# Weight pieces of two chunks' columns for half of the rows, in an attention and SwiGLU kernel

## Chip, cores and metric

The kernel runs on one core of a Trainium2 chip. The metric is the device time of one execution in microseconds (us), the median of three runs; lower is better. The core has five engines with instruction queues of their own: PE (TensorE, with its weight loads listed as PEld), DVE (VectorE), ACT (ScalarE), POOL (GpSimd) and SP (SyncE, which here only starts DMAs).

## What is computed

Block-causal attention over q, k, v of 8 batches, 8 heads, 576 positions and 64 dimensions (float32), then a SwiGLU layer on the 4,608 x 512 result. The three weights are float64.

```python
scores = q @ k.T / sqrt(64)             # hidden where the key's block of 64 is later than the query's
attn = softmax(scores); x = attn @ v    # heads side by side: x is 4608 x 512
g, val = x @ w_gate, x @ w_val          # 512 x 1536 each, float64
out = (g * sigmoid(g) * val) @ w_out    # 1536 x 512, float64
```

## The kernel before

**Work and tiles.** Attention goes by batch and by pairs of heads: scores on PE (L436 in plain float32 for the first two batches, L562 and L646 in split parts after them), copies and masks on ACT (L454, L459), maxima on DVE (L700) and POOL (L704), exponentials on ACT (L732), and the product with v on PE (L772). The first two batches are cut into smaller stretches (`FIRST`). Feed-forward goes by 18 tiles of 256 rows of x; a tile takes the 1,536 columns in 12 chunks of 128, in pairs of chunks. For a pair, `up` makes gate and value products (L1095 to L1097: three products of high and low float32 parts for each of the four row groups d of 128), ACT and DVE make the gated result (L1128 to L1144), and L1186 to L1188 multiply by w_out. Tiles 0 and 1 run between the attention of the first batches, while the weights still come in; `MIXED` gives the order in which their pairs are made.

**Weights.** `weight(i, kind)` brings one piece: chunk i of w_gate, w_val or w_out (kind 0, 1, 2), 36 pieces of 512 KB. A piece of w_gate or w_val is 128 columns for all 512 rows: 128 partitions, four runs of 128 float64 each, so 512 packets of 1,024 bytes. It lands in one of five `wo` buffers (L939). The two words of each float64 are joined into float32 by ACT (L954, L958) and DVE (L963, L968), then split into a high part (ACT, L973) and a low part (DVE, L976), each one instruction of 128x512. They go to `v_all` for w_val, to `g_even` or `g_odd` for w_gate of an even or odd chunk. The loads are chained in the order of chunks and kinds. Copies of the converted w_out are stored to DRAM (L992, L995) for the later tiles.

**Borrowed room.** The copies of w_out chunks 0 to 5 lie, until they are stored and tile 0 (and for chunks 0 to 3 tile 1) has read them, in the room of w_gate chunks 10, 11, 8, 9 and w_val chunks 10, 11 (`AWAY`). The list `before_place` makes the high part of those later pieces wait for that.

**Order.** The order of all instructions is fixed at build time. `add` and `dma` give each task an engine, an estimated cost, a rank and the tasks and buffers that it waits for; `in_order` walks through time and gives an idle engine the ready task of the lowest rank. `PIECES` holds ranks of the weight pieces, `AHEAD` those of some loads, `FIRST` those of attention of batches 0 and 1, `SIDE` those of the products of tiles 0 and 1. A later tile has 10 + its first row / 576, and attention of batch b has 10 + b - `LEAD`, with the score products `EAGER` earlier. `spare` is how far ahead of a buffer's release a task may be queued. Every engine then works through its own list in that order and stands still at an instruction whose inputs aren't there.

Of the kernel before, what the change touches and what calls it, by code (L numbers as in the profile page):

```python
# [7 lines left out]
F32 = mybir.dt.float32  # L8
F32R = mybir.dt.float32r
I32 = mybir.dt.int32  # L10
F16 = mybir.dt.float16
AF = mybir.ActivationFunctionType
ALU = mybir.AluOpType
# [5 lines left out]
def kernel(  # L19
# [17 lines left out]
    nc = tc.nc  # L37
    B, H, S, D = q.shape
    NT, DM = out.shape
    DFF = w_gate.shape[1]  # L40
    P = 128
# [4 lines left out]
    SP = NKC * P  # L46
    NDC = DM // P
# [2 lines left out]
    XT = 256  # L50


    LEAD, EAGER = 1.69, 0.3

    SUMS = 2


    ROWS = (2,)
    MIXED = (0, 0, 1, 1, 0, 1, 0, 0, 1, 1, 0, 1)

    FINE = 4

    AHEAD = {(0, 1): 2.01, (0, 2): 2.07, (1, 0): 2.03, (1, 1): 2.5, (1, 2): 2.5}
    LATER = 0.6

    PIECES = [
        (2.46, 1.85, 2.03),
        (4.86, 5.95, 3.63),
        (4.60, 2.52, 1.48),
        (3.87, 3.06, 5.35),  # L70
        (1.93, 3.59, 2.41),
        (5.14, 6.91, 5.83),
        (3.58, 2.93, 2.93),
        (0.08, 1.36, 0.92),
        (-2.10, -5.86, -4.34),
        (-7.48, -5.87, -3.82),
        (-7.64, -9.14, -8.44),
        (-12.11, -9.50, -10.88),
    ]

    SIDE = (2.98, 4.19)

    PATIENCE = 10.0

    FIRST = {
        0: [(0, 256, (-4.21, 2.41, 2.06, 2.12)), (256, 576, (-2.91, -2.07, -6.62, -4.11))],
        1: [(0, 256, (4.02, 3.94, 4.16, 3.63)), (256, 576, (-2.93, 1.90, 2.56, 4.50))],
    }
    TILES = [XT] * (NT // XT)

# [1 line left out]
    wide = w_gate.dtype != F32  # L92
# [56 lines left out]
    def add(engine, cost, rank, fn, after=(), bufs=(), port=False, mode=""):  # L149


        t = Task(engine, cost, rank, fn, after, bufs, port, mode)
        for a in after:
            if a is not None:
                a.next.append(t)
                t.waits += 1
        for u in bufs:
            u.left += 1
        t.n = len(tasks)
        tasks.append(t)  # L160
        return t


    def act_us(n, psum=False, more=0.0):
        return (0.05 if psum else 0.093) + n * 0.000833 + more

    def dve_us(n, one=False):
        return 0.07 + n * (0.00052 if one else 0.00104)
# [8 lines left out]
    def dma(rank, size, fn, after=(), bufs=(), n=1, engine="SP", packet=1024):  # L177

        t = add(engine, 0.5 * n, rank, fn, after, bufs)
        t.moves = size / packet * (9.0 + 0.0385 * packet) / 16e3  # L180
        return t
# [21 lines left out]
    def w_at(which, x, i):  # L203

        if which:
            return v_all[x][:, :, i * P : (i + 1) * P]
        return (g_odd if i % 2 else g_even)[x][:, :, i // 2 * P : (i // 2 + 1) * P]
# [100 lines left out]
    for i in range(7):  # L308
        n = 2**i
# [31 lines left out]
    def attention(R, b, h, a, e, early, bufs, lane):  # L341
# [1 line left out]

        Q = R - (0.1 if early else EAGER)
        visits, runs = STRETCHES[a, e]
        if b < 2:

# [546 lines left out]
    def words(ap):  # L896
        return ap.bitcast(I32) if wide else ap
# [11 lines left out]
    def weight(i, kind):  # L909

        R = PIECES[i][kind]
        raw = Buf("wo", "raw")
        away = AWAY.get(i) if kind == 2 else None  # L920
        wo = Buf("wo", "out") if kind == 2 and not away else None
        fs = slice(i * P, (i + 1) * P)

        parts = 1 if wo else NDC

        def part(j):
            if wo:
                return wo[0][:, j : j + 1]
            which, c = away or (kind, i)
            return w_at(which, j, c)  # L930

        def load():
            view = raw[0].rearrange("p (n m) -> p n m", n=NDC if kind < 2 else 1)
            if kind < 2:
                fs = slice(i * P * (1 + wide), (i + 1) * P * (1 + wide))
                src = words((w_gate, w_val)[kind])[:, fs].rearrange("(c p) f -> p c f", p=P)
            else:
                src = words(w_out)[i * P : (i + 1) * P, :].rearrange("p (n m) -> p n m", n=1)
            nc.sync.dma_start(out=view, in_=src)  # L939

        t = chain["w"] = dma(AHEAD.get((i, kind), R), 5e5, load, [chain["w"]], [raw], packet=1024 if kind < 2 else 4096)
        bufs = [raw, wo] if wo else [raw]

        def words_of(j):
            w = raw[0].rearrange("p (n t) -> p n t", t=1 + wide)[:, :, j]
            return w.rearrange("p (n m) -> p n m", n=parts)

        y = Buf("ob", "signs") if wide else None


        def signs():
            w = words_of(1).bitcast(F32)
            to = y[0].rearrange("p (n m) t -> p n m t", n=parts)[:, :, :, 1]
            nc.scalar.mul(to, w, 2.0**-60)  # L954

        def scaled():
            w = words_of(1).bitcast(F32)
            nc.scalar.mul(w, w, 2.0**-112)  # L958


        def fraction():
            s = y[0].rearrange("p m t -> p (m t)").bitcast(I32).rearrange("p (n m) -> p n m", n=parts)
            nc.vector.scalar_tensor_tensor(  # L963
                words_of(0), words_of(0), 29, s, ALU.logical_shift_right, ALU.bitwise_or
            )

        def exponent():
            nc.vector.scalar_tensor_tensor(  # L968
                words_of(0), words_of(1), 3, words_of(0), ALU.logical_shift_left, ALU.bitwise_or
            )  # L970

        def high():
            nc.scalar.copy(part(0), words_of(0).bitcast(F32))  # L973

        def low():
            nc.vector.tensor_tensor(  # L976
                part(1), words_of(0).bitcast(F32), part(0).bitcast(F32), ALU.subtract
            )

        if wide:  # L980
            t = add("ACT", act_us(DM, more=0.13), R, signs, [t], [raw, y])
            f = add("DVE", dve_us(DM), R, fraction, [t], [raw, y], True)
            t = add("ACT", act_us(DM, more=0.06), R, scaled, [t], [raw])
            t = add("DVE", dve_us(DM), R, exponent, [t, f], [raw], True)
        t = w_high[i, kind] = add("ACT", act_us(DM, more=0.04), R, high, [t], bufs)
        t = add("DVE", dve_us(DM), R, low, [t], bufs, True)
        if kind == 2:
            w_kept[i] = t, wo, part

            def store():  # L990
                if wo:
                    nc.sync.dma_start(out=wo_d[i], in_=wo[0].bitcast(F32))  # L992
                    return
                for j in range(2):
                    nc.sync.dma_start(  # L995
                        out=wo_d[i][:, j].rearrange("p (n m) -> p n m", n=parts), in_=part(j).bitcast(F32)
                    )

            t = dma(R, 5e5, store, [t], [wo] if wo else [], 2 if away else 1, packet=512 if away else 4096)
            if away:  # L1000
                before_place.append((t, away))
        w_done[i, kind] = t
# [58 lines left out]
    def feed_forward(j, t0, w, xs):  # L1061
# [19 lines left out]
        def up(i, which, prev):  # L1081

            ps = Buf("gv")
            ts = up_done[0]
            for y in range(2):

                for ds in [range(NDC)] if j >= FINE else [[d] for d in range(NDC)]:

                    def products(ds=ds, y=y):
                        hi, lo = (w_at(which, k, i + y) for k in range(2))  # L1090
                        o = ps[0][:, y * w : (y + 1) * w]
                        for d in ds:
                            xhi, xlo = (xs[d][1][k] for k in range(2))
                            first, last = d == 0, d == NDC - 1
                            nc.tensor.matmul(o, lhsT=hi[:, d], rhs=xhi[:, 0:w], start=first, stop=False)  # L1095
                            nc.tensor.matmul(o, lhsT=hi[:, d], rhs=xlo[:, 0:w], start=False, stop=False)  # L1096
                            nc.tensor.matmul(o, lhsT=lo[:, d], rhs=xhi[:, 0:w], start=False, stop=last)  # L1097

                    ts = add(
                        "PE",  # L1100
                        mm_us(w, w, w) * len(ds),
                        rank(i),
                        products,
                        [ts, *(xs[d][0] for d in ds), w_done[i + y, which]],
                        [ps, *(xs[d][1] for d in ds)],
                    )
                    ts.prev = prev
                    prev = ts if j >= FINE else None
            chain["up"] = up_done[0] = ts
            return ps, ts  # L1110
# [161 lines left out]
        next(tiles[j], None)  # L1272

    for t, (which, c) in before_place:
        t.next.append(w_high[c, which])
        w_high[c, which].waits += 1


    IN_TURN = set(
# [3 lines left out]
    def in_order():  # L1283
# [14 lines left out]
        now = queue = 0.0  # L1298
        mode, last = "", None

        spare = {"PE": 2.12, "DVE": 0.32, "ACT": 0.75, "POOL": 0.0, "SP": 0.0}

        def place(t, by):

# [104 lines left out]
```

## Time and profile before

| what | us |
|---|---|
| three runs, median (lowest to highest) | 1179.26 (1177.92 to 1181.79) |
| the profiled execution | 1177.14 |
| its span, first to last instruction | 1175.3 |
| PE busy in the span | 1149.0 |
| DVE, ACT, POOL busy | 754.4, 625.0, 323.7 |

The profiled execution is 1.84 us longer than its span and 2.12 us under the median. PE is busy for 98% of the span, so the time is PE's work and its gaps. The mean granted clock of PE is 0.994 of full speed.

### The profile page before, as it was taken

What the parts mean: (1) busy time and instruction counts of PE and PEld (TensorE: products, weight loads), DVE (VectorE), ACT (ScalarE), POOL (GpSimd) and SP (SyncE); (2) the same over time, 40 slices, a digit from 0 to 9 for tenths busy, and PEclk for the clock granted to TensorE, in tenths of its full rate; (3) what the DMA queues carried; (4) which work ended last, traced back from release to release, by engine and by line L of the source; (5) the groups of instructions that cost most, each with busy time, mean ns of one, the idle gap of its engine ahead of it and who ended that gap; (6) DMA issues with size and microseconds to landing.
All of it is one profiled execution on the core that took longest, in us unless ns stands there. A gap on an engine that the chain in (4) does not pass through costs nothing.

```text
span 1175.3 us, 21803 instructions
## 1 busy us (share of the span) xinstructions
PE 1149.0 (98%) x8512; PEld 1026.9 (87%) x8512; DVE 754.4 (64%) x1226; ACT 625.0 (53%) x1122; POOL 323.7 (28%) x139
## 2 busy tenths in 40 slices
PE   6889999999999999999999999999999999999998
PEld 4568778898898989998999899899989899999997
DVE  5988988575887668768585867686857423323222
ACT  6889877546573837474656565656555212112111
POOL 3222100144535251335233433343324200000000
PEclk9899999999999999999999999999999999999999
DMA  8758756766554756755665565656553536453442
GB/s 213 200 150 217 197 187 227 209 177 166 170 145 139 198 165 167 218 148 158 177 173 153 155 175 146 191 157 173 151 182 125 160 136 190 145 168 135 144 132 102
DMA packets 266983, 197.40 MB, mean 168 GB/s; under 512 B 195264, under 2 KB 231376, under 8 KB 266880
## 3 DMA queue, kind: packets, MB, share of 16 engines
q1 hardware_dynamic: 264304, 195.29, 57.0%
q8 instruction: 67, 1.10, 0.4%
q10 hardware_dynamic: 2576, 0.72, 0.3%
q14 instruction: 36, 0.29, 0.1%
HBM read 171.57 MB, written 24.38 MB: 167 GB/s over the span
## 4 chain that ended last, share of the span: by engine, by line
PE 84%; DVE 6%; ACT 5%; DMA 2%; issue 1%; POOL 1%; SPq 1%; DVEq 0%; ACTq 0%; POOLq 0%
PE gv L1095 16%; PE gv L1097 15%; PE gv L1096 15%; PE po L1186 7%; PE po L1187 7%; PE po L1188 7%; PE at L772 7%; PE at L562 5%; DVE mx L700 1%; DMA wo<-in_moe_w_out_dram 1%; DVE sc L728 1%; PE po L772 1%; PE at L436 1%; ACT sc L732 1%; PE at L646 1%
## 5 line engine op out<-in xcount | busy, mean ns | idle before, releaser
L704 POOL PARTITION_ALL_REDUCE mx<-mx x80 | 142.9, 1833 | 400.4 <-DVE mx L700 126.3
L1095 PE MATMUL gv<-xhl,v_all 128*128 128x256 f32 x864 | 242.3, 280 | 0.8 <-DVE t L1131 0.7
L1097 PE MATMUL gv<-xhl,v_all 128*128 128x256 f32 x864 | 239.7, 277 | 0.2 <-DVE v_all L976 0.2
L1096 PE MATMUL gv<-xhl,v_all 128*128 128x256 f32 x864 | 239.5, 277 | 0.0
L823 POOL PARTITION_ALL_REDUCE mx<-mx x48 | 178.4, 3764 | 195.7 <-DVE mx L700 167.5
L1131 DVE SCALAR_TENSOR_TENSOR t<-t,gv 128x512 f32<-128x512 f32 x108 | 74.0, 685 | 190.4 <-ACT t L1128 190.2
L1095 PEld LDWEIGHTS gv<-xhl,v_all 128*128 128x128 f32 x864 | 162.1, 188 | 5.1 <-issue 2.5
L1096 PEld LDWEIGHTS gv<-xhl,v_all 128*128 128x128 f32 x864 | 162.3, 188 | 0.6
L1097 PEld LDWEIGHTS gv<-xhl,v_all 128*128 128x128 f32 x864 | 162.2, 188 | 0.4 <-DVE v_all L976 0.4
L1128 ACT ACTIVATE t<-gv 128x512 f32<-128x512 f32 x108 | 64.7, 599 | 173.4 <-PE gv L1097 173.3
L1186 PE MATMUL po<-wo,hhl 128*128 128x512 f32 x372 | 147.4, 396 | 0.2 <-ACT ob L1213 0.2
L1187 PE MATMUL po<-wo,hhl 128*128 128x512 f32 x372 | 145.7, 392 | 0.0
L1188 PE MATMUL po<-wo,hhl 128*128 128x512 f32 x372 | 145.1, 390 | 0.2 <-DVE hhl L1144 0.2
L1141 ACT CAST hhl<-t 128x512 fp32r<-128x512 f32 x108 | 67.1, 621 | 130.3 <-DVE t L1136 128.0
L732 ACT ACTIVATE sc<-sc 128x1024 f32<-128x1024 f32 (+3 forms) x104 | 105.9, 1031 | 52.2 <-DVE sc L728 51.5
L1136 DVE SCALAR_TENSOR_TENSOR t<-t,gv 128x512 f32<-128x512 f32 x108 | 73.8, 684 | 90.1 <-PE gv L1097 89.4
L728 DVE TENSOR_TENSOR sc<-sc,mx 128x640 f32<-128x640 f32 (+6 forms) x168 | 122.1, 766 | 13.9 <-POOL mx L704 13.8
L1095 PE MATMUL gv<-xhl,g_even 128*128 128x256 f32 x432 | 123.5, 286 | 0.0
L1097 PE MATMUL gv<-xhl,g_even 128*128 128x256 f32 x432 | 122.2, 283 | 0.0
L1096 PE MATMUL gv<-xhl,g_even 128*128 128x256 f32 x432 | 122.1, 283 | 0.0
L1095 PE MATMUL gv<-xhl,g_odd 128*128 128x256 f32 x432 | 120.8, 280 | 0.0
L1144 DVE TENSOR_TENSOR hhl<-t,hhl 128x512 fp32r<-128x512 f32 x108 | 91.2, 845 | 45.3 <-ACT hhl L1141 44.8
(172 smaller groups left out, 2445.4 us busy)
## 6 DMA issues: line engine op xcount, KB each, us to landing
wo<-wo_d SPq DMA_DIRECT2D x200, 512.0 KB
out_dram<-ob SPq DMA_DIRECT2D x35, 256.0 KB
v<-in_v_dram SPq DMA_DIRECT2D x64, 128.0 KB
xt<-x_d SPq DMA_DIRECT2D x64, 128.0 KB
rt<-r_d SPq DMA_DIRECT2D x128, 64.0 KB
qk<-in_q_dram SPq DMA_DIRECT2D x112, 72.0 KB
qk<-in_k_dram SPq DMA_DIRECT2D x104, 72.0 KB
x_d<-xu SPq DMA_DIRECT2D x24, 288.0 KB
```

Source lines behind the costliest of these rows:

```text
L704: nc.gpsimd.partition_all_reduce(m, m, channels=P, reduce_op=bass_isa.ReduceOp.max)
L728: nc.vector.tensor_tensor(piece(c), scores_of(c), m, ALU.subtract)
L732: nc.scalar.activation(x, x, AF.Exp)
L772: nc.tensor.matmul(ps[0][own(x), 1 - i if sums else i, q0 - s0 : s1 - s0], lhsT=ones if sums else vt[0][:, 2 * lane + c, own(x)], rhs=sc[0 ...
L823: nc.gpsimd.partition_all_reduce(m, m, channels=P, reduce_op=bass_isa.ReduceOp.add)
L1095: nc.tensor.matmul(o, lhsT=hi[:, d], rhs=xhi[:, 0:w], start=first, stop=False)
L1096: nc.tensor.matmul(o, lhsT=hi[:, d], rhs=xlo[:, 0:w], start=False, stop=False)
L1097: nc.tensor.matmul(o, lhsT=lo[:, d], rhs=xhi[:, 0:w], start=False, stop=last)
L1144: nc.vector.tensor_tensor(hh[1][:, 0:n], t[0][:, 0:n], hh[0][:, 0:n].bitcast(F32), ALU.subtract)
L1186: nc.tensor.matmul(po, lhsT=hi, rhs=whi, start=i + y == 0, stop=False)
L1187: nc.tensor.matmul(po, lhsT=hi, rhs=wlo, start=False, stop=False)
L1188: nc.tensor.matmul(po, lhsT=lo, rhs=whi, start=False, stop=i + y == NFC - 1)
```

## The change

Pieces of w_gate and w_val are cut in the other direction: piece i has the columns of both chunks of its pair (256 columns), for the first 256 rows of x's dimension if i is even and the last 256 if it is odd. A piece still has 512 KB, now in 256 packets of 2,048 bytes. For w_gate, the two chunks lie in two tiles, so the high part becomes two ACT instructions and the low part two DVE instructions, of 128x256 each; for w_val they stay one each. Products of row groups d = 0, 1 of either chunk wait for the even piece, those of d = 2, 3 for the odd one. The pieces that come into borrowed room wait for both copies of the pair. The ranks, `MIXED`, `LEAD` and `spare` have new values.

```diff
-    LEAD, EAGER = 1.69, 0.3
+    LEAD, EAGER = 1.50189, 0.3
-    MIXED = (0, 0, 1, 1, 0, 1, 0, 0, 1, 1, 0, 1)
+    MIXED = (0, 0, 1, 1, 0, 0, 1, 0, 1, 1, 1, 0)
-    AHEAD = {(0, 1): 2.01, (0, 2): 2.07, (1, 0): 2.03, (1, 1): 2.5, (1, 2): 2.5}
+    AHEAD = {(0, 1): 2.07, (0, 2): 2.07, (1, 0): 2.07, (1, 1): 2.0, (1, 2): 2.0}
...
-    SIDE = (2.98, 4.19)
+    SIDE = (10.4268, 5.41963)
...
-        Q = R - (0.1 if early else EAGER)
+        Q = R - (0.3 if early else EAGER)
...
+        two = NDC // 2
+        c0, ds = i - i % 2, slice(i % 2 * two, (i % 2 + 1) * two)
...
+        def split(j):
+            if kind == 2:
+                return [(part(j), slice(0, parts), slice(None))]
+            if kind == 1:
+                return [(v_all[j][:, ds, c0 * P : (c0 + 2) * P], slice(0, two), slice(None))]
+            return [(w_at(0, j, c0 + y)[:, ds], slice(0, two), slice(y * P, (y + 1) * P)) for y in range(2)]
...
-                fs = slice(i * P * (1 + wide), (i + 1) * P * (1 + wide))
-                src = words((w_gate, w_val)[kind])[:, fs].rearrange("(c p) f -> p c f", p=P)
+                fs = slice(c0 * P * (1 + wide), (c0 + 2) * P * (1 + wide))
+                src = words((w_gate, w_val)[kind])[:, fs].rearrange("(c p) f -> p c f", p=P)[:, ds]
...
-            nc.scalar.copy(part(0), words_of(0).bitcast(F32))
+            for to, n, m in split(0):
+                nc.scalar.copy(to, words_of(0)[:, n, m].bitcast(F32))
...
-            nc.vector.tensor_tensor(
-                part(1), words_of(0).bitcast(F32), part(0).bitcast(F32), ALU.subtract
-            )
+            for (to, n, m), (hi, *_) in zip(split(1), split(0)):
+                nc.vector.tensor_tensor(to, words_of(0)[:, n, m].bitcast(F32), hi.bitcast(F32), ALU.subtract)
...
-                        [ts, *(xs[d][0] for d in ds), w_done[i + y, which]],
+                        [ts, *(xs[d][0] for d in ds), *{w_done[i + d // 2, which] for d in ds}],
...
     for t, (which, c) in before_place:
-        t.next.append(w_high[c, which])
-        w_high[c, which].waits += 1
+        for x in (w_high[c - c % 2 + d, which] for d in range(2)):
+            t.next.append(x)
+            x.waits += 1
...
-        spare = {"PE": 2.12, "DVE": 0.32, "ACT": 0.75, "POOL": 0.0, "SP": 0.0}
+        spare = {"PE": 1.69146, "DVE": 0.3, "ACT": 0.768518, "POOL": 0.0, "SP": 0.0}
```

All values of `PIECES` and `FIRST` are new too. Of `PIECES`, those of chunks 9 to 11 go from (-7.48, -5.87, -3.82), (-7.64, -9.14, -8.44), (-12.11, -9.50, -10.88) to (1.14, 1.50, 0.81), (8.83, 6.84, 10.33), (-4.23, -3.82, -3.68).

## Rows read from the trace of the kernel before

**Rows 1.** The page, its head and part 1: busy time, share, instructions.

```profile
span 1175.3 us, 21803 instructions
PE 1149.0 (98%) x8512; PEld 1026.9 (87%) x8512; DVE 754.4 (64%) x1226; ACT 625.0 (53%) x1122; POOL 323.7 (28%) x139
```

**Rows 2.** Busy time by stretch: length, engines (instructions), PE's clock, DMA share, GB/s.

```profile
0.00:50.00 50.00, 35.06 (x242) 24.21 (x244) 36.15 (x85) 37.78 (x70) 16.44 (x22) 0.90 0.80 207
...
62.00:70.00 8.00, 4.69 (x31) 2.75 (x31) 7.90 (x15) 7.04 (x15) 0.58 (x1) 0.89 0.34 71
...
130.00:150.00 20.00, 18.76 (x129) 14.61 (x128) 17.18 (x29) 16.33 (x30) 2.76 (x2) 1.00 0.76 214
150.00:160.00 10.00, 8.17 (x63) 5.81 (x61) 7.97 (x18) 5.94 (x12) 0.00 (x0) 1.00 0.56 177
...
sum 200.00, PE 178.37 PEld 138.63 DVE 167.18 ACT 158.44 POOL 43.28; mean PE 25.48 PEld 19.80 DVE 23.88 ACT 22.63 POOL 6.18
```

**Rows 3.** The same view in steps of 2 us, one step.

```profile
68.00:70.00 2.00, 1.50 (x6) 0.77 (x8) 2.00 (x4) 2.00 (x6) 0.00 (x0) 0.57 0.77 155
```

**Rows 4.** Timeline of PE, two like groups of products: start us, us, what.

```profile
57.16 2.27 PE L772 MATMUL po<-sc,v 128*64 128x320 f32 x20
...
68.50 3.83 PE L772 MATMUL at<-sc,v 128*64 128x320 f32 x20 [1.11 <-ACT sc L459]
```

**Rows 5.** The chain that ended last, in order of time: start us, us, what.

```profile
30.05 0.56 ACT g_even L973
...
132.56 5.96 DMA wo<-in_moe_w_out_dram
...
147.47 0.61 DVE g_even L976
148.10 5.74 DMA wo<-in_moe_w_out_dram
```

**Rows 6.** DMA queue, 155 to 156.5 us, then 1154 to 1156: packets, MB, share.

```profile
q1 hardware_dynamic: 534, 0.52, 100.0%
...
q1 hardware_dynamic: 195, 0.73, 101.6%
```

**Rows 7.** Groups by shape to 200 us (mean ns); lines L330, L333 (min/median/max ns).

```profile
L973 ACT CAST g_even<-wo 128x512 fp32r<-128x512 f32 x8 | 5.4, 674 | 0.8 <-DVE wo L968 0.8
...
L976 DVE TENSOR_TENSOR g_even<-wo,g_even 128x512 fp32r<-128x512 f32 x8 | 5.5, 685 | 0.7 <-ACT g_even L973 0.7
...
L330 ACT CAST xhl<-xt x72: 389/408/450, 21.8 to 1071.2; 128x256 fp32r<-128x256 f32 x72
...
L333 DVE TENSOR_TENSOR xhl<-xt,xhl x72: 361/419/2751, 22.9 to 1071.6; 128x256 fp32r<-128x256 f32 x72
```

**Rows 8.** Line L1188 to 205 us, then ACT's timeline: the room of chunk 8.

```profile
L1188 PE MATMUL po<-g_even,hhl x4: 389/392/397, 89.7 to 145.1; 128*128 128x512 f32 x4
L1188 PE MATMUL po<-g_odd,hhl x4: 394/397/397, 91.4 to 146.9; 128*128 128x512 f32 x4
...
145.58 0.68 ACT L973 CAST g_even<-wo 128x512 fp32r<-128x512 f32 x1
```

**Rows 9.** Lines L884 and L1042 (first and last start), then a late stretch.

```profile
L884 SPq DMA_DIRECT2D x_d<-xu x36: 320/442/1207, 52.4 to 927.5; - x36
...
L1042 SPq DMA_DIRECT2D xt<-x_d x64: 319/382/1250, 106.2 to 1068.5; - x64
...
1000.00:1050.00 50.00, 50.00 (x366) 47.05 (x365) 15.55 (x26) 9.98 (x18) 0.00 (x0) 1.00 0.48 158
```

**Rows 10.** Timeline of SP: two weight loads with none between them.

```profile
54.09 0.42 SPq L939 DMA_DIRECT2D wo<-in_moe_w_gate_dram  x1
...
68.38 0.46 SPq L939 DMA_DIRECT2D wo<-in_moe_w_val_dram  x1
```

**Rows 11.** Timeline 153 to 160 us: ACT, then PE, held up.

```profile
153.86 0.79 ACT L954 ACTIVATE ob<-wo 128x512 f16<-128x512 f32 x1 [2.34 <-DMA wo<-in_moe_w_out_dram]
...
155.72 0.81 PE L436 MATMUL at<-parts,parts 64*128 64x320 f32 x4 [1.11 <-ACT xu L787]
```

More of the change, by code (lines that the diff above doesn't have):

```diff
@@ L50 @@
     XT = 256
-    LEAD, EAGER = 1.69, 0.3
+    LEAD, EAGER = 1.50189, 0.3
     SUMS = 2
     ROWS = (2,)
-    MIXED = (0, 0, 1, 1, 0, 1, 0, 0, 1, 1, 0, 1)
+    MIXED = (0, 0, 1, 1, 0, 0, 1, 0, 1, 1, 1, 0)
     FINE = 4
-    AHEAD = {(0, 1): 2.01, (0, 2): 2.07, (1, 0): 2.03, (1, 1): 2.5, (1, 2): 2.5}
+    AHEAD = {(0, 1): 2.07, (0, 2): 2.07, (1, 0): 2.07, (1, 1): 2.0, (1, 2): 2.0}
     LATER = 0.6
     PIECES = [
[L67 to L78, printed above, removed]
+        (2.63882, 1.07212, 4.68676),
+        (5.50618, 7.57593, 4.09145),
+        (5.62103, 4.05549, 2.87636),
+        (4.69475, 1.70596, 6.37759),
+        (1.61696, 2.48245, 2.33394),
+        (3.93856, 7.47651, 7.97263),
+        (6.41623, 5.61484, 5.86523),
+        (1.54421, -0.468471, 4.29014),
+        (-3.07897, -6.96645, -1.77202),
+        (1.14037, 1.50068, 0.811512),
+        (8.8289, 6.84027, 10.3309),
+        (-4.23089, -3.81584, -3.6848),
     ]
-    SIDE = (2.98, 4.19)
+    SIDE = (10.4268, 5.41963)
     PATIENCE = 10.0
     FIRST = {
-        0: [(0, 256, (-4.21, 2.41, 2.06, 2.12)), (256, 576, (-2.91, -2.07, -6.62, -4.11))],
-        1: [(0, 256, (4.02, 3.94, 4.16, 3.63)), (256, 576, (-2.93, 1.90, 2.56, 4.50))],
+        0: [(0, 256, (-2.92219, 2.54558, 2.22979, 2.29361)), (256, 576, (-0.267482, 1.25775, -5.48701, -2.49645))],
+        1: [(0, 256, (2.59521, 0.70283, 2.60847, 3.90476)), (256, 576, (-7.58039, -2.65868, 1.92199, 3.74629))],
     }
@@ L921, in weight @@
         wo = Buf("wo", "out") if kind == 2 and not away else None
-        fs = slice(i * P, (i + 1) * P)
         parts = 1 if wo else NDC
+        two = NDC // 2
+        c0, ds = i - i % 2, slice(i % 2 * two, (i % 2 + 1) * two)
         def part(j):
@@ L928, in part @@
                 return wo[0][:, j : j + 1]
-            which, c = away or (kind, i)
-            return w_at(which, j, c)
+            return w_at(away[0], j, away[1])
+        def split(j):
[4 more added lines that the diff above has]
+            return [(w_at(0, j, c0 + y)[:, ds], slice(0, two), slice(y * P, (y + 1) * P)) for y in range(2)]
         def load():
-            view = raw[0].rearrange("p (n m) -> p n m", n=NDC if kind < 2 else 1)
+            view = raw[0].rearrange("p (n m) -> p n m", n=two if kind < 2 else 1)
             if kind < 2:
-                fs = slice(i * P * (1 + wide), (i + 1) * P * (1 + wide))
-                src = words((w_gate, w_val)[kind])[:, fs].rearrange("(c p) f -> p c f", p=P)
+                fs = slice(c0 * P * (1 + wide), (c0 + 2) * P * (1 + wide))
+                src = words((w_gate, w_val)[kind])[:, fs].rearrange("(c p) f -> p c f", p=P)[:, ds]
             else:
@@ L939, in load @@
             nc.sync.dma_start(out=view, in_=src)
-        t = chain["w"] = dma(AHEAD.get((i, kind), R), 5e5, load, [chain["w"]], [raw], packet=1024 if kind < 2 else 4096)
+        t = chain["w"] = dma(AHEAD.get((i, kind), R), 5e5, load, [chain["w"]], [raw], packet=2048 if kind < 2 else 4096)
         bufs = [raw, wo] if wo else [raw]
@@ L945, in words_of @@
             w = raw[0].rearrange("p (n t) -> p n t", t=1 + wide)[:, :, j]
-            return w.rearrange("p (n m) -> p n m", n=parts)
+            return w.rearrange("p (n m) -> p n m", n=parts if kind == 2 else two)
+        n_signs = parts if kind == 2 else two
         y = Buf("ob", "signs") if wide else None
@@ L952, in signs @@
             w = words_of(1).bitcast(F32)
-            to = y[0].rearrange("p (n m) t -> p n m t", n=parts)[:, :, :, 1]
+            to = y[0].rearrange("p (n m) t -> p n m t", n=n_signs)[:, :, :, 1]
             nc.scalar.mul(to, w, 2.0**-60)
@@ L961, in fraction @@
         def fraction():
-            s = y[0].rearrange("p m t -> p (m t)").bitcast(I32).rearrange("p (n m) -> p n m", n=parts)
+            s = y[0].rearrange("p m t -> p (m t)").bitcast(I32).rearrange("p (n m) -> p n m", n=n_signs)
             nc.vector.scalar_tensor_tensor(
@@ L984, in weight @@
             t = add("DVE", dve_us(DM), R, exponent, [t, f], [raw], True)
-        t = w_high[i, kind] = add("ACT", act_us(DM, more=0.04), R, high, [t], bufs)
-        t = add("DVE", dve_us(DM), R, low, [t], bufs, True)
+        t = w_high[i, kind] = add("ACT", act_us(DM, more=0.04 if kind else 0.13), R, high, [t], bufs)
+        t = add("DVE", dve_us(DM) + (0.0 if kind else 0.07), R, low, [t], bufs, True)
         if kind == 2:
```

## The prediction

> **What bounds the kernel now.** I read the page's head first: PE is busy for 1149.0 of 1175.3 us, so 26.3 us of PE's time is idle [rows 1]. The second view, busy time by stretch, says where. Up to 200 us PE is busy for 178.37, so 21.6 of the 26.3 us are there; 14.9 are in the first 50 us, 3.3 between 62 and 70, 1.2 between 130 and 150 and 1.8 between 150 and 160 [rows 2]. The other 4.7 us lie after it and are spread over 975 us, the end among them, so there is next to nothing to win there, as long as x and weights come in time. The stage to look at is that of the weights, and there three engines are short at once: in the 8 us of the hole at 62, DVE is busy for 7.90 and ACT for 7.04, while the DMA share is 0.34 [rows 2]. DMA isn't what PE misses there; no weight load starts between 54.09 and 68.38 [rows 10].
>
> The clock adds to a hole. From 68 to 70 us the granted clock is 0.57, so most of that stretch is at the lower of the two levels, 1.2 GHz [rows 3]; ahead of it PE was idle for much of 62 to 68. Twenty products of L772 then take 3.83 us where the like group took 2.27 at full clock [rows 4], so this hole costs another 1.6 us.
>
> The third view is the chain of waits. In the first 200 us it goes by turns over ACT, DVE, PE and DMA. Two of its longest links are loads of w_out, 5.96 and 5.74 us; and eight instructions that split w_gate pieces into high and low parts stand on it, three on ACT and five on DVE, the first at 30.05 and the last at 147.47 [rows 5]. What such a late load does is seen at 153.86: ACT stands still for 2.34 us at a weight's first step, with the copy out of PSUM queued behind it, and PE then waits 1.11 us for that copy [rows 11].
>
> **The change, part by part.**
>
> *Packets.* In a stretch where nearly all packets have 1,024 bytes and the engines are full, 534 packets take 16 x 1.5 us, 45 ns each, and the 0.52 MB make 46 us of engine time per MB. In a full stretch of 4,096-byte packets it is 16 x 2 x 1.016 us for 0.73 MB, 44.5 us per MB [rows 6]. No 2,048-byte load is in the trace, so it lies between these by size: a saving of 0 to 4%. A piece takes 512 x 45 / 16 = 1.44 us of the queue, so 0 to 0.06 us are saved on it, 0 to 1.4 us on 24 pieces. Nearly all of that is queue time beside other work. On the path are the two w_out loads of the chain; if one piece of the new kind is still ahead of each in the queue, that is 2 x 0.06, so -0.1 us. I take that end, since 2,048 lies halfway between the two rows (twice the one, half the other) and the term is small either way.
>
> The Trainium skill, DMA: Bandwidth & Descriptors, Specifications, gives 512 bytes as the least transfer that reaches the line rate. By that rule packets of 1,024 bytes are already there and the term would be 0, the sum below 0.1 us higher. The trace's 4% between 1,024 and 4,096 bytes stands near that rule.
>
> *Two instructions for one.* Each of the 12 w_gate pieces has its cast and its subtraction in two halves of 128x256. The nearest rows of that size are L330, 0.408 us on ACT, and L333, 0.419 on DVE; the whole ones take 0.674 and 0.685 [rows 7]. So a piece costs ACT 2 x 0.408 - 0.674 = 0.14 us more and DVE 2 x 0.419 - 0.685 = 0.15 more: 1.7 and 1.8 us in all, on engines that are the pace up to 160 us. If all lies under other work it is 0, if nothing does 3.5. On the chain as it stands are three and five: 3 x 0.14 + 5 x 0.15 = 1.2 us, which I take.
>
> *Waiting for the pair.* The bytes needed for a whole pair of chunks are the same, but the even piece alone now allows only row groups 0 and 1, half of what a w_gate piece allowed to the chunk's products. PE's waits in this stage are for attention, so I take 0. Borrowed room is another matter. The high part of w_gate chunk 8 is cast at 145.58, right after the last read of the w_out copy in its room, 145.1; the copy in chunk 9's room is read until 146.9 [rows 8]. The new piece 8 waits for both: up to 1.8 us later, with its `wo` buffer held and what stands behind it in ACT's list. ACT is idle for 4.1 of the 10 us from 150 [rows 2], so most is covered; I take +0.4, between 0 and 1.8. The five other pieces in borrowed room get the same rule.
>
> *Ranks.* This is the largest term and the trace can only bound it. The gain can't be more than the holes outside the start, 3.3 + 1.2 + 1.8 = 6.3 us [rows 2], with the 1.6 us of the clock: -7.9. A worse order could open holes of the same kind and size: +7.9. What speaks for a gain is `SIDE`: products of tile 0 get 10.43 for 2.98, behind all attention of batches 0 and 1, so they are kept for moments in which attention waits. In the trace PE is full from 50 to 62 and then starves for 3.3 us. What speaks against a large one: in that hole DVE and ACT are nearly full, so the attention that PE waits for can't come much sooner; the products of tile 0 only change places. I take half of the holes, -3.2 us, and nothing for the clock.
>
> `LEAD` falls from 1.69 to 1.50, so attention of each batch comes 0.19 batch later. The last piece of x is stored at 927.5. The last tile's x is loaded from about 1068.5, and a tile's 360 products take 49 us at 366 in 50 us [rows 9], so tile 15, the first that needs batch 7 and two tiles before, loads at some 970. That leaves 42 us, of which 0.19 of a batch (2.25 tiles of 49 us, so 21 us, an estimate without the attention between them) is given up. It stays hidden: 0.
>
> **Sum.** -0.1 + 1.2 + 0.4 - 3.2 = -1.7 us on the profiled 1177.14, so 1175.4; the median of the runs is 2.1 above the profiled one, so 1177.5.
>
> **Rivals.**
>
> *Tile 0 as filler closes the holes (faster).* If its products are there when the attention of batches 0 and 1 waits, all 6.3 us go and the slow stretch with them: -0.1 + 1.2 + 0.4 - 7.9 = -6.4, so 1172.9. For it: 12 us of full PE right ahead of a hole. Against it: DVE and ACT, which get 3.5 us more work.
>
> *The pair rule holds up the last pieces (slower).* Tile 0 comes later by its new rank, and with it the reads of the six borrowed copies, for which now both pieces of a pair wait, two of the five `wo` buffers in hand. Then loads of the last chunks start late, as at 148.10 [rows 5], and ACT stands at each as at 153.86 [rows 11]. One such case costs PE the 1.8 us of 150 to 160; with four of them the time is 4 x 1.8 + 1.2 = 8.4 us longer, 1187.7. It decides from the point at which chunk 8's cast is later than ACT's 4.1 us of slack cover, that is past 150 us by the times of now. Against it: ranks can put other work there.
>
> *The order is worse by itself (slower).* One more hole like that at 62, with its slow clock, and the extra instructions: 3.3 + 1.6 + 1.2 = 6.1, 1185.4.
>
> *The packets do nothing.* Then the only gain is from the order, and the sum moves by 0.1; it lies inside the forecast.
>
> **How the numbers follow.** A measurement of this kernel tells about 0.3%, 3.5 us, from no change. The forecast (1177.5, own range 1175.7 to 1182.8, within 0.3%) has 0.38; the filler rival 0.34; the pair rule 0.17; the worse order 0.11. So faster 0.34, same 0.38, slower 0.28. The range takes in the filler rival and, with the unknown ends of the extra instructions (3.5 for 1.2) and of the holes in the start, goes to 1169 below and 1189 above.
>
> **What would show it.** Right: the splits of w_gate in halves of about 0.41 us each; pieces of w_gate that land no sooner; PE's idle time up to 200 us between 18 and 22 us; no wait on x after 200 us. The filler rival: PE idle for under 17 us up to 200, no slow stretch between 60 and 75. The pair rule: ACT or DVE standing at a weight piece of chunks 8 to 11, and PE idle for more than 5 us between 130 and 210. I would be wrong altogether if PE's busy time changed by more than 2 us, or if the time moved after 200 us.

## The result, and the profile after

| kernel | median us (lowest to highest), runs | profiled execution | span | PE busy |
|---|---|---|---|---|
| before | 1179.0 (1177.55 to 1181.79), 11 | 1177.14 | 1175.3 | 1149.0 |
| changed | 1182.5 (1180.71 to 1185.21), 11 | 1182.78 | 1181.0 | 1150.3 |

The changed kernel is slower: ratio 1.0032, 95% interval 1.0023 to 1.0040, so 3.8 us (2.7 to 4.7). I had forecast 1.7 us faster. The head of its page, to be read beside [rows 1]:

```profile
span 1181.0 us, 21817 instructions
...
PE 1150.3 (97%) x8512; PEld 1028.1 (87%) x8512; DVE 760.4 (64%) x1238; ACT 622.2 (53%) x1134; POOL 322.9 (27%) x139
```

The span is 5.7 us longer and PE's work 1.3 us, so PE's idle time goes from 26.3 to 30.7 us: +4.4. The view by stretch, of the changed kernel, with columns as in [rows 2], in two answers:

```profile
62.00:70.00 8.00, 8.00 (x71) 5.93 (x71) 7.27 (x14) 7.81 (x16) 2.70 (x2) 1.00 0.72 187
70.00:90.00 20.00, 15.67 (x138) 12.06 (x134) 18.78 (x39) 18.79 (x43) 5.47 (x4) 1.00 0.65 179
130.00:140.00 10.00, 8.12 (x64) 5.90 (x62) 6.94 (x15) 8.21 (x16) 3.11 (x2) 1.00 0.81 245
160.00:170.00 10.00, 8.60 (x68) 6.84 (x67) 10.00 (x21) 8.41 (x15) 0.00 (x0) 1.00 0.47 161
200.00:220.00 20.00, 18.27 (x132) 15.77 (x131) 13.18 (x22) 11.95 (x22) 1.27 (x1) 1.00 0.73 225
...
200.00:300.00 100.00, 97.14 (x741) 85.47 (x740) 74.17 (x114) 58.71 (x100) 37.07 (x14) 1.00 0.68 189
0.00:200.00 200.00, 175.98 (x1291) 135.39 (x1292) 166.20 (x329) 157.00 (x308) 44.56 (x43) 0.96 0.70 193
```

And the kernel before, in four of the same stretches:

```profile
70.00:90.00 20.00, 19.73 (x169) 15.26 (x166) 16.66 (x33) 15.55 (x36) 6.19 (x6) 0.96 0.58 181
...
160.00:170.00 10.00, 10.00 (x76) 9.40 (x75) 9.00 (x15) 6.69 (x11) 2.76 (x2) 1.00 0.28 83
200.00:220.00 20.00, 20.00 (x144) 16.67 (x144) 13.35 (x26) 10.09 (x21) 0.00 (x0) 1.00 0.56 162
...
200.00:300.00 100.00, 99.61 (x769) 87.28 (x769) 68.57 (x114) 57.20 (x99) 30.85 (x12) 1.00 0.65 178
```

The hole at 62 is closed, as the filler rival had it: PE is busy for 8.00 of 8 us there, 4.69 before [rows 2]. But one of 4.3 us has come between 70 and 90, and others of 1.4 and 1.7 us at 160 and 200, where PE was full before. Up to 200 us PE is idle for 24.0 us against 21.6; from 200 to 300, where I had expected no change, 2.9 us against 0.4. So the holes moved and grew.

What holds the late pieces up shows in three views of the changed kernel: reads of the w_out copies in the room of w_gate chunks 8 and 9, ACT's timeline, SP's timeline.

```profile
L1201 PE MATMUL po<-g_even,hhl x4: 388/395/397, 105.0 to 154.2; 128*128 128x512 f32 x4
...
L1201 PE MATMUL po<-g_odd,hhl x4: 392/395/398, 107.8 to 156.8; 128*128 128x512 f32 x4
```

```profile
157.01 0.41 ACT L987 CAST g_even<-wo 128x256 fp32r<-128x256 f32 x1
157.32 0.42 ACT L987 CAST g_odd<-wo 128x256 fp32r<-128x256 f32 x1
157.65 0.43 ACT L987 CAST g_even<-wo 128x256 fp32r<-128x256 f32 x1
157.97 0.43 ACT L987 CAST g_odd<-wo 128x256 fp32r<-128x256 f32 x1
```

```profile
134.31 1.41 SPq L951 DMA_DIRECT2D wo<-in_moe_w_gate_dram  x1
...
148.64 0.51 SPq L951 DMA_DIRECT2D wo<-in_moe_w_gate_dram  x1
...
161.44 0.37 SPq L951 DMA_DIRECT2D wo<-in_moe_w_val_dram  x1
...
177.32 0.38 SPq L951 DMA_DIRECT2D wo<-in_moe_w_gate_dram  x1
...
202.71 0.34 SPq L951 DMA_DIRECT2D wo<-in_moe_w_out_dram  x1
```

Tile 0 reads the second copy until 156.8; only then are both pieces cast, 8 and 9 back to back. Piece 8 was loaded from 134.31, so it held a `wo` buffer for over 20 us. The cast of chunk 8 was at 145.58 before [rows 8]. The next load, the w_val piece 9, waits until 161.44 (SP stands for 8.2 us, released by a subtraction into `g_even`), and the last load starts at 202.71, 7.6 us later than before. The same three loads in the kernel before (w_val piece 9, w_gate piece 10, the last w_out piece) are these:

```profile
164.19 0.37 SPq L939 DMA_DIRECT2D wo<-in_moe_w_val_dram  x1
...
172.49 0.38 SPq L939 DMA_DIRECT2D wo<-in_moe_w_gate_dram  x1
...
195.07 0.33 SPq L939 DMA_DIRECT2D wo<-in_moe_w_out_dram  x1
```

So the load that waits for the pair is not late: it starts 2.8 us sooner than it did before. The loads fall behind after it, by 4.8 us at w_gate piece 10. ACT stands still at weight loads for 12.4 us up to 215 us, in 8 cases, against 5.4 us in 4 (one of these in [rows 11]):

```profile
ACT ob L967 <- DMA wo<-in_moe_w_out_dram: 6.0, 4, 3.3
ACT ob L967 <- DMA wo<-in_moe_w_gate_dram: 4.8, 3, 2.2
ACT ob L967 <- DMA wo<-in_moe_w_val_dram: 1.6, 1, 1.6
```

(What waited, for what: us in total, cases, longest.) Which of this costs the time was left to experiments.

### The profile page after: what moved, and what is told of

Its sections match the earlier page's. It is cut to its first block, busy times and chain, and to the rows that moved or that the text cites. A ratio compares the mean times of both kernels' runs of the same rounds, so it can differ in the third digit from the quotient of the medians.

```text
span 1181.0 us, 21817 instructions
## 1 busy us (share of the span) xinstructions
PE 1150.3 (97%) x8512; PEld 1028.1 (87%) x8512; DVE 760.4 (64%) x1238; ACT 622.2 (53%) x1134; POOL 322.9 (27%) x139
## 4 chain that ended last, share of the span: by engine, by line
PE 86%; ACT 5%; DVE 4%; DMA 3%; issue 1%; POOL 1%; SPq 0%; DVEq 0%; ACTq 0%; POOLq 0%
PE gv L1108 16%; PE gv L1110 16%; PE gv L1109 16%; PE po L1199 7%; PE po L1201 7%; PE po L1200 7%; PE at L772 7%; PE at L562 6%; DVE sc L728 1%; DMA wo<-in_moe_w_out_dram 1%; ACT sc L732 1%; ACT sc L454 1%; PE at L646 1%; POOL mx L704 1%; DMA wo<-in_moe_w_gate_dram 1%
## 5 line engine op out<-in xcount | busy, mean ns | idle before, releaser
L728 DVE TENSOR_TENSOR sc<-sc,mx 128x640 f32<-128x640 f32 (+6 forms) x168 | 126.3, 792 | 25.2 <-POOL mx L704 24.2
L1108 PE MATMUL gv<-xhl,g_odd 128*128 128x256 f32 x432 | 120.9, 280 | 0.0
L1110 PE MATMUL gv<-xhl,g_odd 128*128 128x256 f32 x432 | 119.6, 277 | 0.0
```

Of the source, the lines that this page charges most:

```text
L728: nc.vector.tensor_tensor(piece(c), scores_of(c), m, ALU.subtract)
```

## The experiments

Two theories stood against each other. One: the pieces themselves cost the time (more instructions, the pair rule, later landing). Two: the new ranks give a worse order. Since a changed wait or cost also changes the planned order, some of the kernels keep an order and change only what is done in it; where ranks or waits change, the order is planned anew. Times are medians; ratios are against the kernel before on the same chip.

### The new order with the old pieces

The changed kernel, planned as it is, with loads and casts of before:

```diff
-                src = words((w_gate, w_val)[kind])[:, fs].rearrange("(c p) f -> p c f", p=P)[:, ds]
+                fs = slice(i * P * (1 + wide), (i + 1) * P * (1 + wide))
+                src = words((w_gate, w_val)[kind])[:, fs].rearrange("(c p) f -> p c f", p=P)
...
-            for to, n, m in split(0):
-                nc.scalar.copy(to, words_of(0)[:, n, m].bitcast(F32))
+            nc.scalar.copy(part(0), words_of(0).bitcast(F32))
```

> The order, the waits and the buffers of the changed kernel, instruction by instruction; only what a w_gate or w_val piece holds is as before (one chunk, 1,024-byte packets, casts and subtractions of 128x512 in one instruction). If the pieces themselves cost the time (12 more instructions on ACT and DVE each, 0.23 + 0.16 us a piece by the trace of the changed kernel), it comes back to 1179 to 1180. If the packets help and the halves lie under other work, it is slower than 1182.5, by up to 2 us. If the order is what costs, it stays at 1182.5, within 1.

1181.0 us, ratio 1.0011 (1.0003 to 1.0019). About a third of the loss is there without the new pieces; the rest, 2.5 us by the two ratios, goes with the pieces (0.9 us by the second measurement of the changed kernel below). The last loads of SP in this kernel, and ACT's cast of chunk 8, stand at

```profile
159.93 0.37 SPq L952 DMA_DIRECT2D wo<-in_moe_w_val_dram  x1
...
175.94 0.38 SPq L952 DMA_DIRECT2D wo<-in_moe_w_gate_dram  x1
...
201.40 0.34 SPq L952 DMA_DIRECT2D wo<-in_moe_w_out_dram  x1
```

```profile
157.05 0.65 ACT L987 CAST g_even<-wo 128x512 fp32r<-128x512 f32 x1
```

The last load is 1.3 us before that of the changed kernel and 6.3 us after that of the kernel before, and the cast is as late as in the changed kernel. So most of the lateness belongs to the order. So does the hole between 70 and 90: from 75 to 100 us PE is idle for 2.5 us in this kernel, 2.7 in the changed one and 0.3 in the one before.

### The new ranks alone, the new pieces alone

The kernel before with the new constants; the changed kernel with the old ones.

> The kernel before with the new constants alone (ranks, LEAD, MIXED, AHEAD, SIDE, FIRST, spare, the 0.3 for the early scores); pieces and waits as before. If the new order is what costs, 1182 to 1183. If the pieces and their pair rule are what costs, 1179, within 1.

> The changed pieces, packets and pair rule with all constants as before. If the pieces and the pair rule cost the 3.5 us, 1182 to 1183. If the order of the new ranks does, 1179 to 1180. If the old ranks fit the old waits only, so that the order falls apart under the new ones, above 1184.

1184.0, ratio 1.0037 (1.0023 to 1.0052), and 1189.3, ratio 1.0093 (1.0075 to 1.0110). Neither theory gives both. The new ranks lose with the old pieces too, and the old ranks lose much more under the new waits and costs. The new ranks win back some 7 us of what the new pieces lose with the old ranks; they don't win anything against the old kernel. The twelve runs of the first of these kernels go from 1178.1 to 1188.9, so one fixed order can itself vary by 11 us from run to run.

### The pair rule, then the new pieces under it, with the old ranks

The old constants, costs and waits, to which the new waits are added; then the same order with the new pieces.

```diff
-                        [ts, *(xs[d][0] for d in ds), *{w_done[i + d // 2, which] for d in ds}],
+                        [ts, *(xs[d][0] for d in ds), *{w_done[i + x, which] for x in {y, *(d // 2 for d in ds)}}],
```

> The kernel before, constants and pieces as before, with the new waits added to the old ones: both w_gate or w_val pieces of a pair in borrowed room wait for both w_out copies of that pair, and products wait for the pieces of old and new rule. The order is planned anew under these waits. My 0.4 us for the pair rule gives 1179.4. The pair rule as the main cost (four held-up pieces of 1.8 us) gives 1183 or more.

> Constants as before, the pair rule added to the old waits, order and buffers exactly those of the run with that rule and old pieces (1180.3), now with the new pieces. If the new pieces cost the 1.5 to 2.5 us that they cost under the new order, 1182 to 1183. If that cost belongs to the new order alone, 1180 to 1181.

1180.3, ratio 1.0006 (0.9998 to 1.0015), so the rule costs 0.7 us with the order that it leads to, and no cost at all lies within the interval (-0.2 to 1.8 us). With the new pieces 1182.8, ratio 1.0030 (1.0019 to 1.0041): 2.4 parts in a thousand more, 2.8 us, in the same order. Compared with the run above (1189.3), which has the same pieces and ranks and differs only in the planner's costs (three constants of 0.07 to 0.14 us) and in the old waits that are added here, it is 6.5 us faster: that much hangs on the order alone.

### The changed kernel again, and parts of the new pieces in its order

```diff
+            for n in [slice(0, 2), slice(2, 4)] if kind == 0 else [slice(None)]:
+                nc.scalar.copy(part(0)[:, n], words_of(0)[:, n].bitcast(F32))
```

> The changed kernel as it is, beside the next three on one chip. 1182 to 1183 against 1179 to 1180 of the kernel before.

> Order, waits and buffers of the changed kernel and pieces as before (1,024-byte packets, one chunk), but each w_gate piece cast and subtracted in two instructions of 128x256 (two row groups each). The same order with whole instructions took 1181.0, the changed kernel 1182.5. If the second instruction of the halves is what the new pieces cost, this is as slow as the changed kernel, 1182 to 1183. If the cost comes from the packets or from where the bytes lie, 1181, within 0.5.

> Order, waits and buffers of the changed kernel, with the new pieces for w_val alone (2,048-byte packets, two chunks, one instruction) and w_gate pieces as before. If packets of 2,048 bytes save 0.06 us a piece and no more, 1181, within 0.5, as with all pieces old. If they were a gain on the path, 1180 or less. If they are a loss (later landing, nearer to the changed kernel), 1182 or more.

The changed kernel gave 1182.6, ratio 1.0019 (1.0009 to 1.0028), lower than the first time: two measurements of one kernel can lie a thousandth apart. Halves alone: 1.0017 (1.0007 to 1.0027). New w_val pieces alone, where only packets and layout differ: 1.0018 (1.0005 to 1.0031). All old was 1.0011. The intervals overlap, so which part costs is inconclusive; the 2,048-byte packets show no gain, though one as small as the forecast 0.1 us could not be seen here.

### Halves in the old order

The edit shown above, in the kernel before.

> The kernel before, order, packets and waits kept, with each w_gate piece cast and subtracted in two instructions of 128x256. My step gave 1.2 us for this, between 0 and 3.5: 1180.4. If halves are free, 1179.2; if all of them lie on the path, 1182 to 1183.

1179.9, ratio 1.0004 (0.9995 to 1.0014): 0.5 us by the ratio (-0.6 to 1.7). The second instructions are cheap; the interval holds both no cost and my 1.2.

### ACT's stands at late loads

The planned order, with the first step of the pieces at which ACT stood put later (the lines are those of the kernel before, with its four pieces):

```diff
+    LATE, STANDS = {}, {(2, 1): 1.5, (7, 1): 0.9, (7, 2): 1.8, (8, 2): 2.7}
...
+                t.key = now + LATE.get(t, 0.0)
```

> The changed kernel with its planned order, in which the first step (ACT) of the seven weight pieces at which ACT stood still for 0.9 to 3.3 us in its trace is put 1.6 to 3.6 us later in the order, with what depends on it, so that other work of ACT goes first. Ranks, waits and buffers as planned. If ACT standing at late loads is what the new order lost against the old one (12.4 us of it against 5.4), this is back at 1179 to 1180.5. If it isn't on the way to PE, 1182 to 1183. If the late conversion is missed elsewhere, above 1184.

> The same for the kernel before, for the four pieces at which ACT stood for 0.5 to 2.3 us. If standing at loads is what opens the holes of PE at 138 and 154, 1176 to 1178. If not, 1179 to 1180.

1182.0, ratio 1.0020 (1.0011 to 1.0028), and 1182.0, ratio 1.0022 (1.0010 to 1.0033). The stands are gone, in the changed kernel 12.4 us of them but for

```profile
ACT ob L969 <- DMA wo<-in_moe_w_gate_dram: 1.0, 1, 1.0
ACT ob L969 <- DMA wo<-in_moe_w_val_dram: 0.6, 1, 0.6
```

and it is as slow as in its second measurement; the kernel before became 2.6 us slower. So taking the stands away gives nothing back in the sum. What later conversions cost elsewhere is in that sum too, so this doesn't show that a stand costs nothing. At one place the trace shows what one costs, the hole at 160. In the changed kernel, ACT at the load of w_gate piece 9, then PE:

```profile
153.50 0.79 ACT L967 ACTIVATE ob<-wo 128x512 f16<-128x512 f32 x1 [1.39 <-DMA wo<-in_moe_w_gate_dram]
...
163.16 0.81 PE L436 MATMUL at<-parts,parts 64*128 64x320 f32 x4 [1.40 <-ACT sc L459]
```

The same two in the same order with the old pieces, where neither waits:

```profile
152.05 0.80 ACT L968 ACTIVATE ob<-wo 128x512 f16<-128x512 f32 x1
...
161.74 0.81 PE L436 MATMUL at<-parts,parts 64*128 64x320 f32 x4
```

Between them, DVE waits 1.10 us for that step of ACT, and its subtraction of the maximum starts at 158.71 instead of 157.27. In the second profile of the changed kernel ACT stands for 1.25 us and PE for 1.3, with the halves alone 0.97 and 1.0, with the new w_val pieces alone neither does. In each of these five profiles of one order PE loses what ACT stood. Why the load is late in three of them isn't shown.

### SIDE alone, both ways

> The kernel before with the new SIDE alone (10.43 and 5.42 for 2.98 and 4.19), so that tile 0's products give way to all attention of the first two batches. My prediction took this as the lever of the new ranks, worth about -3: 1176. If the other ranks were fitted to the old SIDE, the order comes apart and it is slower, 1182 to 1190.

> The changed kernel with the old SIDE (2.98, 4.19) and all else new. If keeping tile 0's products back is a gain of its own, as I had it, this is slower than the changed kernel by about 3 us: 1185 to 1186. If SIDE only fits its set, it is slower too, by as much as any change of a fitted rank does (the nudges: 0 and 11 us). If the new SIDE is a loss in itself, faster, 1179 to 1181.

| | old SIDE | new SIDE |
|---|---|---|
| old constants and pieces | 1179.8 | 1189.2 |
| new constants and pieces | 1186.4 | 1182.6 |

The new `SIDE` in the old set costs 9.4 us (1.0079, 1.0066 to 1.0092), the old one in the new set some 4 (1.0058, 1.0039 to 1.0078, against 1.0019 to 1.0032 for the changed kernel). The first shows that it is no lever; the second was forecast as slower by either reading, so it tells nothing more. That the value fits its set is what the two together suggest.

### Nudges that mean nothing

```diff
-        (2.46, 1.85, 2.03),
-        (4.86, 5.95, 3.63),
+        (2.4738, 1.8603, 2.0268),
+        (4.8504, 5.9505, 3.6262),
```

> The kernel before with every number of PIECES and SIDE moved by a random amount up to 0.02 either way, which means nothing in itself. If the time hangs on the meaning of the ranks, 1179 to 1180. If it hangs on the exact order that the planner happens to give, several us slower: 1182 to 1190.

> A second random draw of up to 0.02 either way on every number of PIECES and SIDE of the kernel before. If the order's luck is what moves the time, again slower, though by another amount: 1180 to 1190. If the first draw was an odd case, 1179 to 1180.

1190.7, ratio 1.0093 (1.0080 to 1.0107), and 1179.4, ratio 1.0001 (0.9990 to 1.0011). In these two draws a change of ranks by up to 0.02 costs 11 us or nothing. The first draw's stretches from 150 us:

```profile
150.00:200.00 50.00, 45.88 (x334) 38.54 (x333) 42.74 (x72) 33.05 (x55) 5.77 (x5) 0.96 0.49 152
200.00:250.00 50.00, 45.95 (x301) 36.72 (x301) 34.57 (x59) 30.88 (x55) 5.33 (x3) 0.98 0.71 200
```

PE is idle for 8.2 us there, 2.0 before. In this trace too the weights come late: the last load starts at 210.3, against 195.1 before.

### What sets the pace of the stage

One step of attention taken nearly away in the first two batches, in the old order: DVE's subtraction, then ACT's exponential.

```diff
-                nc.vector.tensor_tensor(piece(c), scores_of(c), m, ALU.subtract)
+                n = slice(0, 8) if b < 2 and not stays else slice(None)
+                nc.vector.tensor_tensor(piece(c)[:, :, n], scores_of(c)[:, :, n], m[:, :, n], ALU.subtract)
```

> The kernel before, its order kept, with the subtraction of the maximum (L728) in the first two batches done on 8 columns only where it works in place; the rest of the scores stays unreduced. That takes some 26 of the 31 us that these 48 instructions have on DVE up to 200 us. If DVE's pace makes PE's holes, 3 to 8 us faster, 1171 to 1176. If the weights' loads and buffers make them, under 2 us faster.

> The kernel before, its order kept, with the exponential (L732) of the first two batches on 8 columns of each call only; the other scores go into the product with v as they are. That takes some 25 of the 28 us that these 32 instructions have on ACT up to 200 us. If ACT's pace makes PE's holes, 3 to 8 us faster, 1171 to 1176. If loads and buffers make them, under 2 us faster.

1178.1, ratio 0.9991 (0.9980 to 1.0003), and 1175.9, ratio 0.9970 (0.9958 to 0.9982). Their sums up to 300 us, DVE's lighter kernel first:

```profile
sum 300.00, PE 277.75 PEld 226.35 DVE 215.75 ACT 215.83 POOL 72.29; mean PE 46.29 PEld 37.73 DVE 35.96 ACT 35.97 POOL 12.05
```

```profile
sum 300.00, PE 276.14 PEld 225.49 DVE 235.42 ACT 196.80 POOL 74.77; mean PE 46.02 PEld 37.58 DVE 39.24 ACT 32.80 POOL 12.46
```

Up to 300 us the kernel before has 235.74 us on DVE and 215.64 on ACT, so 20.0 us went from DVE and 18.8 from ACT, less than the 26 and 25 that sums of records had promised. DVE's part brings 1.1 us, and no gain lies within its interval. ACT's brings 3.5 us (2.1 to 5.0), within the band that was named for ACT's pace. So ACT's pace is a part of what makes the holes, at about 0.2 us for each us taken away, and DVE's alone isn't seen to be. PE's idle time up to 300 us, 22 and 24 us against 22 before, can't be set against this: the executions profiled took 1176.63 and 1178.04 us, the second 2.1 above its median. What makes the rest of the holes, the weights' loads and the five `wo` buffers among the candidates, was not tested.

### LEAD alone

> The kernel before with LEAD of 1.50 for 1.69 alone: attention from batch 2 on comes 0.19 batch later in the order. By my reading its slack of 42 us covers that: 1179 to 1180. If LEAD is what costs PE 2 us between 200 and 250 in the changed kernel, 1181 to 1182.

1178.0, ratio 0.9985 (0.9974 to 0.9996). The later attention costs nothing with the old ranks, as I had it, so PE's loss after 200 us is hardly from `LEAD`. It is if anything 1.8 us faster than the kernel before, the only kernel here that does all the work and is; the interval ends close to 1, and I wouldn't build on it.

## Why the prediction was wrong

**The ranks, -3.2 us: the step that failed.** I counted the holes and had the new `SIDE` close half of them. The largest did close, and the time came back at 70, 160 and 200 us. With the old pieces the new order takes 1.3 us more than before; 0.7 of that is what the pair rule costs the old ranks, so the ranks are worth about +0.6 in place of -3.2, an error of 3.8 us of the 5.5 by which the forecast missed. Both measured terms have about 1 us of room either way, and with the old waits the same ranks cost 4.4 us (1184.0); no run has them as a gain over the kernel before. The reasoning was wrong in kind: it took one rank for a lever with a meaning. The table of `SIDE` and the nudges show that one constant can't be taken out of its set, and that a neighbouring order can be 11 us worse. I take the constants to be fitted together; then a set found anew for other pieces has no reason to beat a set fitted to the old ones. What it did is win back what the new waits and costs break (1189.3 to 1182.5).

**The pace.** I argued that DVE and ACT are the pace of the stage, since both were nearly full in the hole. Taking 20 us from DVE gave 1.1 us or nothing, taking 19 from ACT gave 3.5. So it holds in part for ACT, and isn't borne out for DVE, though DVE is the fuller of the two in the hole. That an engine is full beside a hole doesn't make it the cause.

**Two instructions for one, +1.2.** The mechanism is right; the size was too large by what the trace shows, in two ways. I took durations of records, but back-to-back instructions overlap. In the rows above the four casts start 0.31 to 0.33 us apart, so a pair takes 0.64 of ACT, and a whole cast 0.55 (from 145.58 [rows 8] to the next start at 146.13). On DVE, in the changed kernel and then in the one before:

```profile
160.66 0.42 DVE L991 TENSOR_TENSOR g_even<-wo,g_even 128x256 fp32r<-128x256 f32 x1
160.99 0.42 DVE L991 TENSOR_TENSOR g_odd<-wo,g_odd 128x256 fp32r<-128x256 f32 x1
161.33 0.42 DVE L991 TENSOR_TENSOR g_even<-wo,g_even 128x256 fp32r<-128x256 f32 x1
```

```profile
147.39 0.68 DVE L976 TENSOR_TENSOR g_even<-wo,g_even 128x512 fp32r<-128x512 f32 x1
147.99 0.68 DVE L963 SCALAR_TENSOR_TENSOR wo<-wo,ob 128x512 int32<-128x512 int32 x1
```

A pair 0.67, a whole one 0.60. So 0.09 and 0.07 us a piece, not 0.14 and 0.15. The Trainium skill, ScalarE: Activation LUTs, What ACT_TABLE_LOAD costs, gives 186 ns of fixed time for an ACTIVATE with immediate scale and bias and an overlap of about 93 ns, so about 93 ns for a second one as an estimate. The trace's casts agree, with 0.09 us.

I also miscounted. Two of the eight instructions that I took for splits of w_gate split w_out pieces, whose copies lie in borrowed room and stay in one instruction. The cast into `g_even` at 30.05 [rows 5] is that of w_out chunk 0: of w_gate only chunks 0 and 1 were loaded by then, chunk 0 was cast at 16.78, and chunk 1 goes to `g_odd`. The subtraction at 96.78 in that chain is that of w_out chunk 4, since SP stores the copy as soon as the cast before it is done (ACT, then SP):

```profile
95.33 0.68 ACT L973 CAST g_even<-wo 128x512 fp32r<-128x512 f32 x1
...
96.03 1.74 SPq L995 DMA_DIRECT2D wo_d<-g_even  x2
```

That leaves two casts and four subtractions on the chain: 2 x 0.09 + 4 x 0.07 = 0.5 us, and 0.9 at my own prices. Halves in the old order measured 0.5 (-0.6 to 1.7), which agrees with either.

**The packets, -0.1.** No gain, as near as can be told. Full and nearly full stretches of the DMA queue in the changed kernel, 181 to 182.5 and 93.5 to 95 us, mostly 2,048-byte packets:

```profile
q1 hardware_dynamic: 303, 0.60, 104.7%
...
q1 hardware_dynamic: 162, 0.31, 74.5%
```

That is 1.047 x 24 / 0.60 = 42 and 0.745 x 24 / 0.31 = 58 us of engine time per MB; 1,024-byte packets took 46 in [rows 6] and, from 165 to 166.5 in the kernel before,

```profile
q1 hardware_dynamic: 314, 0.32, 76.0%
```

57. The spread within one size is larger than between the sizes. New w_val pieces alone measured nothing better.

**The pair rule, +0.4.** By itself it measured 0.7 (-0.2 to 1.8) with the old ranks. In the new order the first part of my slower rival came: chunk 8 is cast at 157.01, past the 150 from which I had it decide, with two pieces in hand. Its price of 8.4 us did not come. The order with the old pieces has that cast at 157.05 and takes 1181.0, and the load that waited starts no later than before. What the rule costs there wasn't measured apart. What I missed is that the time of that cast hangs on when tile 0 reads the copies, which the ranks set.

**What is left.** New pieces in a fixed order cost 2.8 us with the old ranks and 1 to 2.5 with the new; by the old order the halves explain about 0.5. Products that wait for a split are not it, as I had it with my 0: PE waits for one once up to 300 us in the changed kernel, for 0.3 us. One place is seen, the hole at 160, 1.0 to 1.4 us in the three profiles with halved w_gate pieces in the new order and absent in the two without; the medians of whole runs don't separate these kernels. What the rest is stays open: packets alone and halves alone can't be told from the old pieces within their intervals. The terms as measured, 0.7 for the pair rule, 0.6 for the ranks and some 2 for the pieces, make 3.3 of 3.8 us.

**The signs that I named.** PE is idle for 24.0 us up to 200, outside my 18 to 22, and the time moved after 200 us too (PE's idle time there goes from 4.7 to 6.7 us), which I had said would make me wrong altogether; no wait on x came there, and the halves take 0.41 to 0.43 us each, as forecast. Of the pair rule's signs one came, ACT standing at four pieces of chunks 9 to 11, and one nearly: PE is idle for 4.7 us between 130 and 210, where I had named 5. The rival of a worse order comes nearest, with its new hole between 70 and 90, but the clock stayed at 1.00 there, and its 1185.4 was too slow. PE's busy time changed by 1.3 us, under the 2 that I allowed. 1182.5 lies within the range of 1169 to 1189; the sign was missed because the term with the widest bounds, -7.9 to +7.9, also carried the sign.

## What to carry to other kernels

In a kernel whose order is planned from fitted constants, price an edit by keeping the order and changing the work, and the order by nudging the constants at random: here the first gave 0.5 to 3 us and the second 0 to 11. Don't credit a refit with the holes it could close; it starts by paying for what the edit broke. Add the distance between starts, not the length of records, for instructions that come back to back.

## What was not expected of the hardware

A 512 KB load takes far longer than its 1.4 us of queue: where ACT waited for one, it lay 4.0 to 6.1 us from issue to first use. In the changed kernel that is 148.64 to 153.50 and 177.32 to 183.30 with 2,048-byte packets, and 164.64 to 168.60 and 202.71 to 208.80 with 4,096; in the kernel before 44.43 to 48.91 with 1,024. Two casts that follow each other cost 0.09 us more than one of the same size in all, where their records say 0.14.
